# Attention chunks of 480, 480, 448 and 448 queries, a spread of the v and z preparation, and later read-back of the logits, in an attention and mixture-of-experts kernel

## The chip, the cores and the metric

One core of a Trainium2 chip runs the whole kernel. The metric is device time in microseconds (us). The engines are TensorE (PE, with its weight loads as PEld), VectorE (DVE), ScalarE (ACT), GpSimd (POOL) and SyncE (SP), which issues most of the DMAs.

## The reference

Eight batches of 1856 positions with 256 features: an attention without softmax, multiplied with `u`, and then a mixture of experts (MoE) with 4 groups of 4 experts over all 14848 rows.

```python
scores = z @ z.T / S                      # z: (8, 1856, 64)
attn = np.maximum(scores, 0.0) ** 2
x = (u * (attn @ v)).reshape(N, 256)      # N = 14848
g_idx = argmax(x @ w_group)               # g_w, e_w: softmax weights of the chosen
e_idx = argmax(x[g_idx == g] @ w_expert[g])
h = np.maximum(x @ w1[g, e], 0.0)         # 256 -> 1024
out = g_w * e_w * (h @ w2[g, e])          # 1024 -> 256
```

## The kernel before

**Precision.** Every product runs in split form: a value is cut into a high part, which ACT or DVE rounds to the matmul's type, and a low part, which DVE forms as the difference. So `v` becomes `vh` and `vl` (L246, L247), `z` becomes `z2h` and `z2l` (L215, L216), and the attention weights become `ah` and `al` (L275, L278).

**Attention** (about 10 to 892 us) runs over 8 batches, 4 query chunks and 15 key blocks of 128 keys (the last one holds 64 keys, high and low part packed together). The chunks are the list `QW`: 512, 512, 512 and 320 queries, from the offsets `QO`. One step `s` is one key block of one chunk. Keys are numbered through: step 60·b + 15·c + k is key k of chunk c in batch b, and names such as `al_293` carry that number. `scores(s)` makes two matmuls into a PSUM bank (L265, L266), with `zm`, the chunk's own queries, as the moving operand; ACT takes the relu (L268) and the square (L274), DVE casts `ah` and subtracts `al`. For the keys in `ACT_TWICE` ACT squares twice and DVE has no cast. `attn_v(s)` makes six matmuls (L295, L296, L298) into two accumulating banks, four for the last key. `scores` runs five steps (`LEAD`) ahead of `attn_v`.

**The end of a chunk** (`chunk_end`): DVE multiplies with `u` (`xT`), ACT and DVE cut the result (`xh`, `xl`), ACT copies it into 16-bit planes (`pl`, L336), SP transposes these with DMAs into `rows` (L342). Four matmuls make the routing logits (L350, L351), ACT copies them to `lgp` (L355), SP transposes them by DMA to `lgx` (L358), and DVE copies them back to `lgf` (L364, `logits_tr`, deferred by 5 steps). From there the generator `route` yields small DVE operations, three per step, makes three small matmuls and ends with POOL's scatters of rows into DRAM buckets (L480). A chunk whose width is no multiple of 128 has a partial tile: POOL then clears the rest of `pl` and `lgp` (L328, L329), and planes and `lgp` are copied in two pieces.

**Preparation of the next batch.** `prep_z` loads a block of 512 (the last: 320 and the tail) columns of z (L208, L210) and later cuts it; `prep_v` loads 512 rows of v (L234, L240) and later cuts them; `prep_zm` copies the queries of the next chunk from `z2h` and `z2l` to `zm` (L225, L226). Rings of buffers bound how early that can be: two for raw v, two for raw z, which `lgp` shares, sixteen for cut v (two batches).

**Batch 0** has 16 prefills besides (L661, one for each expert's bucket, 1280 rows of 264 words, 1.35 MB each), which SP issues.

**What sets the order.** A scheduler with a cost model orders each engine's instructions within the dependencies and the rings, so the place in the program is a wish: loads and cuts of v and z go where their buffers come free.

**The MoE** (from about 892 us) runs expert by expert in blocks of up to 512 rows: `phase1` (L616 to L618) with the block's width as columns, `phase2` (L639, L640). The change doesn't touch it.

Of the kernel before, what the change touches and what calls it, by code (L numbers as in the profile page):

```python
# [19 lines left out]
P = 128  # L20
# [4 lines left out]
def f32(ap):  # L25
    return ap.bitcast(F32)
# [3 lines left out]
def tile_glu_attn_moe(  # L30
# [19 lines left out]
    TAIL = S - NKF * P  # L50
    NK = NKF + 1
    assert TAIL == 64 and DQ == 64 and ND == 2 and NE == 16
    NQ = 4
    QW = [512, 512, 512, S - 1536]
    QO = [0, 512, 1024, 1536]
    assert all(cv % 16 == 0 and cv >= 2 * P for cv in caps)
    assert 256 <= QW[3] and QW[3] + TAIL <= 512
    RW = D + 8
    RU = 2 * RW
    CAPB = (N + 511) // 512 * 512 + 512  # L60
# [40 lines left out]
    def bank(pl, tag, name):  # L101
        return pl.tile([P, 512], F32, tag=tag, name=name)

    bucket = tc.dram_tile([NROW + OVT, RW], I32, name="bucket")
    views = dram_disjoint_views(bucket, B * NK)

    padrow = cst("padrow", [P, RW], I32)
    nc.gpsimd.memset(padrow, 0)
# [6 lines left out]
        out=tri, in_=tri, compare_op=ALU.is_gt, fill=0.0, base=0,  # L115
# [73 lines left out]
    def defer(step, fn):  # L189
        deferred.append((step, fn))  # L190
# [8 lines left out]
    bz = {}  # L199
# [1 line left out]
    zms = {}  # L201

    def prep_z(b, c):
        q0, w = QO[c], QW[c]
        wx = w + (TAIL if c == NQ - 1 else 0)
        zr = sb("zr", [P, 512], F32, 2, f"zr_{b}_{c}")
        for h in range(2):
            nc.sync.dma_start(zr[h * DQ:(h + 1) * DQ, 0:w], zT[b, :, q0:q0 + w])  # L208
            if wx > w:
                nc.sync.dma_start(zr[h * DQ:(h + 1) * DQ, w:wx], zT[b, :, S - TAIL:S])  # L210

        def split():
            z2h = new_z(f"z2h_{b}_{c}")
            z2l = new_z(f"z2l_{b}_{c}")
            nc.scalar.copy(out=z2h[:, 0:wx], in_=zr[:, 0:wx])  # L215
            nc.vector.tensor_sub(out=z2l[:, 0:wx], in0=zr[:, 0:wx], in1=f32(z2h[:, 0:wx]))  # L216
            bz[(b, c)] = (z2h, z2l)

        return split

    def prep_zm(b, c):
        w = QW[c]
        z2h, z2l = bz[(b, c)]
        zm = sb("zm", [P, 512], F32R, 2, f"zm_{b}_{c}")
        nc.vector.tensor_copy(out=zm[0:DQ, 0:w], in_=f32(z2h[0:DQ, 0:w]))  # L225
        nc.vector.tensor_copy(out=zm[DQ:P, 0:w], in_=f32(z2l[DQ:P, 0:w]))  # L226
        zms[(b, c)] = zm

    def prep_v(b, c):
        n = min(4, NK - 4 * c)  # L230
        nfull = min(n, NKF - 4 * c)
        raw = new_stg(f"vr_{b}_{c}")
        rv = raw.rearrange("p (k d) -> p k d", d=D)
        nc.sync.dma_start(  # L234
            rv[:, 0:nfull, :],
            v[b, 4 * c * P:(4 * c + nfull) * P, :].rearrange("(k p) d -> p k d", p=P),
        )
# [12 lines left out]
        return split  # L250
# [140 lines left out]
    def route(b, c, rows, lg, nt, part):  # L391
        NG = nt * 5

        def t(tag, shape, dt=F32):
# [29 lines left out]
            out=oh16.rearrange("p i (g e) -> p i g e", e=4),  # L424
# [13 lines left out]
        for _ in range(4):  # L438
# [10 lines left out]
            out=rk, in0=pk[:, 0:W].rearrange("p (i e) -> p i e", e=NE),  # L449
# [128 lines left out]
    wts = {}  # L578
# [90 lines left out]
    pz = prep_z(0, 0)  # L669
    pv = prep_v(0, 0)  # L670
# [20 lines left out]
    for s in range(NS):  # L691
        b, c, k = steps[s]
        if s == 1:
            pv1()
        if s in (0, 4):
            n0 = s // 4 + 2
            pz1 = prep_z(0, n0)
            pv2.append(prep_v(0, n0))
        if s in (2, 6):
            pz1()  # L700
        if s in (5, 9):
            pv2.pop(0)()
        if b == 0 and s >= 10 and s % 2 == 0 and s < 10 + 2 * NE:
            prefill((s - 10) // 2)
        nxt = s // NK + 1
        if k == 0:
            if nxt < B * NQ:
                load_ut(nxt // NQ, nxt % NQ)
            if b + 1 < B:
                if c < NQ - 1:  # L710
                    pv = [prep_v(b + 1, c)]
            else:
                if c == 0:
                    wts[0] = new_w("e0")
                pv = []
                if c:
                    pv = [load_w(regs(0)[0], wts[0], c - 1, "e0")]
                if c == NQ - 1:
                    pv.append(load_w(regs(0)[0], wts[0], c, "e0"))
        for zc, zb, lc, lk, sk in ((0, b + 1, 2, 0, 4), (1, b + 1, 3, 0, 4), (2, b + 1, 3, 6, 10), (3, b, 0, 0, 4)):  # L720
            if c == lc and 0 < zb < B:
                if k == lk:
                    pz = prep_z(zb, zc)
                if k == sk:
                    pz()
        if k == 12 and b + 1 < B and c == NQ - 2:
            pv.append(prep_v(b + 1, NQ - 1))
        if k in (11, 13) and pv:
            pv.pop(0)()
        if k == 8 and nxt < B * NQ and (nxt // NQ, nxt % NQ) in bz:  # L730
# [12 lines left out]
        run_gens(s, 3)
# [52 lines left out]
    def ot(shape, name, dt=F32):  # L796
# [24 lines left out]
        out=big, in0=exc.unsqueeze(2).to_broadcast([P, NE, TOV]),  # L821
# [115 lines left out]
```

## Time and profile before

| what | value |
|---|---|
| median of three runs | 1595.3 us (1595.13 to 1595.54) |
| the profiled execution, its own time | 1597.17 us |
| its span in the profile | 1595.3 us |
| attention, from the trace | about 10 to 892 us |
| MoE | about 892 us to the end |
| mean granted clock of PE | 0.993 |

A window of the trace gives, for a stretch, each engine's busy time and number of instructions. Since matmuls are pipelined, a full PE shows as busy throughout; where an engine is below the length of its stretch, it waited. The timeline gives each instruction with the idle time ahead of it and what released it, in square brackets.

### The profile page before, as it was taken

To read this page: it belongs to the slowest core of one execution; us is meant where nothing else is said; L and a number is where in the kernel's file an instruction comes from. 1 tells how busy PE (TensorE), PEld (TensorE's weight loads), DVE (VectorE), ACT (ScalarE), POOL (GpSimd) and SP (SyncE) were. 2 spreads that over 40 slices of the span, in tenths; PEclk is the share of its full clock that TensorE was granted. 3 is DMA by queue.
4 is the path that set the end of the run, shared out by engine and by line. 5 is a ranking of instruction groups with operands and counts; after the bars stand their busy time and mean duration, and the time that the engine had idled before them with its cause. 6 is when DMAs were issued, how large, how long until landed. Compare 5 with 4: busy or idle time off the path is not lost.

```text
span 1595.3 us, 23282 instructions
## 1 busy us (share of the span) xinstructions
PE 1549.9 (97%) x7808; PEld 1311.1 (82%) x7808; DVE 1081.1 (68%) x2539; ACT 1000.0 (63%) x1886; POOL 273.0 (17%) x323
## 2 busy tenths in 40 slices
PE   8998989999999999999999999999999999999998
PEld 5777877878878878878888798988888888888887
DVE  6868777787787786878787846555555555555572
ACT  6877778887787878787888535344444444444432
POOL 0003211111121211121202321112112222111211
PEclk9999999999999999999999999999999999999999
DMA  8794233233151333231332454233333433333200
GB/s 262 245 297 138 73 89 82 78 104 82 45 142 45 88 102 77 81 85 48 93 91 68 122 109 126 81 100 106 100 96 92 103 102 89 83 91 112 78 23 20
DMA packets 245115, 161.55 MB, mean 101 GB/s; under 512 B 168939, under 2 KB 224243, under 8 KB 244992
## 3 DMA queue, kind: packets, MB, share of 16 engines
q1 hardware_dynamic: 233296, 129.14, 31.8%
q0 software_dynamic: 11696, 30.90, 5.7%
q8 instruction: 62, 1.02, 0.3%
q14 instruction: 61, 0.50, 0.1%
HBM read 72.50 MB, written 53.59 MB: 79 GB/s over the span
## 4 chain that ended last, share of the span: by engine, by line
PE 77%; issue 6%; DVE 5%; ACT 5%; DMA 4%; SPq 2%; POOL 1%; POOLq 0%; ACTq 0%; DVEq 0%
PE py L639 13%; PE o L295 9%; PE o L296 9%; PE o L298 9%; PE py L640 7%; PE ph L617 6%; PE ph L616 6%; PE ph L618 6%; PE sc L265 5%; PE sc L266 5%; DMA lgx<-lgp 1%; SPq L661 1%; ACT r L268 1%; DVE al L278 1%; ACT r L274 1%
## 5 line engine op out<-in xcount | busy, mean ns | idle before, releaser
L295 PE MATMUL o<-ah,vl 128*128 128x512 f32 (+1 forms) x960 | 358.8, 375 | 12.1 <-DVE ah L275 12.1
L296 PE MATMUL o<-ah,vh 128*128 128x512 f32 (+1 forms) x960 | 356.8, 373 | 0.0
L639 PE MATMUL py<-w_e,hh 128*128 128x512 f32 (+3 forms) x1024 | 348.3, 394 | 0.0
L268 ACT ACTIVATE r<-sc 128x512 f32<-128x512 f32 (+1 forms) x480 | 255.7, 554 | 123.8 <-PE sc L266 86.6
L278 DVE TENSOR_TENSOR al<-r,ah 128x512 fp32r<-128x512 f32 (+1 forms) x448 | 285.2, 638 | 39.0 <-ACT r L272 31.8
L298 PE MATMUL o<-al,vh 128*128 128x512 f32 (+1 forms) x896 | 279.8, 378 | 17.8 <-DVE al L278 17.5
L640 PE MATMUL py<-w_e,hl 128*128 128x256 f32 (+4 forms) x1024 | 264.7, 280 | 0.1
L622 DVE SCALAR_TENSOR_TENSOR hl<-ph,hh 128x512 fp32r<-128x512 f32 (+10 forms) x288 | 175.0, 615 | 119.8 <-ACT hh L621 119.3
L621 ACT ACTIVATE hh<-ph 128x512 fp32r<-128x512 f32 (+10 forms) x288 | 153.5, 538 | 151.7 <-PE ph L618 150.0
L480 POOL DMA_INDIRECT bucket<-rows,di x120 | 127.6, 1063 | 564.0 <-issue 245.7
L647 POOL DMA_INDIRECT out_dram<-y,meta x128 | 129.4, 1011 | 552.3 <-DVE y L645 526.7
L295 PEld LDWEIGHTS o<-ah,vl 128*128 128x128 f32 x960 | 182.5, 190 | 48.7 <-DVE ah L275 19.3
L274 ACT ACTIVATE r<-r 128x512 f32<-128x512 f32 (+1 forms) x384 | 219.5, 591 | 3.1
L639 PEld LDWEIGHTS py<-w_e,hh 128*128 128x128 f32 (+3 forms) x1024 | 181.4, 185 | 36.7
L617 PE MATMUL ph<-xh_m,w1h_e 128*128 128x512 f32 (+10 forms) x576 | 207.7, 361 | 0.0
L616 PE MATMUL ph<-xh_m,w1l_e 128*128 128x512 f32 (+10 forms) x576 | 207.4, 360 | 0.0
L298 PEld LDWEIGHTS o<-al,vh 128*128 128x128 f32 x896 | 164.5, 191 | 52.2 <-DVE al L278 26.3
L618 PE MATMUL ph<-xl_m,w1h_e 128*128 128x512 f32 (+10 forms) x576 | 206.3, 361 | 0.0
L296 PEld LDWEIGHTS o<-ah,vh 128*128 128x128 f32 x960 | 182.5, 190 | 28.3
L640 PEld LDWEIGHTS py<-w_e,hl 128*128 128x128 f32 (+4 forms) x1024 | 187.6, 185 | 11.3 <-DVE hl L622 0.5
L275 DVE CAST ah<-r 128x512 fp32r<-128x512 f32 (+1 forms) x384 | 152.1, 399 | 55.8 <-ACT r L274 55.5
L265 PE MATMUL sc<-zm,z2h 128*128 128x512 f32 (+1 forms) x480 | 180.7, 384 | 6.6 <-ACT r L268 4.8
(140 smaller groups left out, 1862.2 us busy)
## 6 DMA issues: line engine op xcount, KB each, us to landing
raw_e<-in_w_dram SPq DMA_DIRECT2D x64, 512.0 KB, 3.9
bucket<-padrow SPq DMA_DIRECT2D x16, 1320.0 KB, 14.0
vr<-in_v_dram SPq DMA_DIRECT2D x24, 512.0 KB, 4.7
ut<-in_uT_dram SPq DMA_DIRECT2D x24, 512.0 KB, 4.0
zr<-in_zT_dram SPq DMA_DIRECT2D x48, 128.0 KB, 2.7
ut<-in_uT_dram SPq DMA_DIRECT2D x8, 320.0 KB, 3.2
vr<-in_v_dram SPq DMA_DIRECT2D x8, 256.0 KB, 3.4
out_dram<-y,meta POOLq DMA_INDIRECT x128, 2.4
```

What stands on the lines that cost most here:

```text
L265: nc.tensor.matmul(ps[:, 0:w], z2h[:, ks], zm, start=True, stop=False)
L268: nc.scalar.activation(out=a, in_=ps[:, 0:w], func=AF.Relu, scale=1.0 / S)
L274: nc.scalar.activation(out=a, in_=a, func=AF.Square)
L278: nc.vector.tensor_sub(out=al, in0=a, in1=f32(ah))
L295: nc.tensor.matmul(o, vl[:, dsl], ah, start=(k == 0), stop=False)
L296: nc.tensor.matmul(o, vh[:, dsl], ah, start=False, stop=(k == NK - 1))
L298: nc.tensor.matmul(o, vh[:, dsl], al, start=False, stop=False)
L616: nc.tensor.matmul(o, wt["l"][d][:, fs], xh[:, d, 0:W], start=(d == 0), stop=False)
L617: nc.tensor.matmul(o, wt["h"][d][:, fs], xh[:, d, 0:W], start=False, stop=False)
L618: nc.tensor.matmul(o, wt["h"][d][:, fs], xl[:, d, 0:W], start=False, stop=(d == ND - 1))
L639: nc.tensor.matmul(py[0:m], hh[:, ts], w2t, start=(f == 0), stop=False)
L640: nc.tensor.matmul(py[0:m, 0:D], hl_[:, ts], w2t[:, 0:D], start=False, stop=(f == NF - 1))
```

## The change

The four chunks become 480, 480, 448 and 448 wide, from 0, 480, 960 and 1408. The z blocks keep their 512 columns (`ZW`), so that `prep_zm` copies a chunk's queries out of one or two z blocks in two to four pieces. Every chunk now has a partial tile, of 96 or 64 rows, and four row tiles. `ACT_TWICE` goes from three keys to two. The loads and cuts of the next batch's v and z follow the table `PREP`, whose entries are a kind, a block, and two places (chunk, key) for load and cut. The logits' copy `lgf` is deferred by 8 steps in place of 5, except for the very last chunk. In the views for the scatters each chunk has `NT` = 4 of its own.

```diff
-    QW = [512, 512, 512, S - 1536]
-    QO = [0, 512, 1024, 1536]
+    QW = [480, 480, 448, 448]
+    QO = [0, 480, 960, 1408]
+    ZW = [512, 512, 512, S - 1536]
...
-    ACT_TWICE = (3, 7, 11)
+    ACT_TWICE = (4, 10)
+    NT = 4
...
 def prep_z(b, c):
-        q0, w = QO[c], QW[c]
+        q0, w = 512 * c, ZW[c]
...
 def prep_zm(b, c):
+        q = QO[c]
+        while q < QO[c] + QW[c]:
+            n = min(512 * (q // 512 + 1), QO[c] + QW[c]) - q
+            z2h, z2l = bz[(b, q // 512)]
+            src, dst = slice(q % 512, q % 512 + n), slice(q - QO[c], q - QO[c] + n)
+            nc.vector.tensor_copy(out=zm[0:DQ, dst], in_=f32(z2h[0:DQ, src]))
+            nc.vector.tensor_copy(out=zm[DQ:P, dst], in_=f32(z2l[DQ:P, src]))
+            q += n
...
-        defer(s + 5, logits_tr)
-        gens.append((max(s + 6, 42), g))
+        wait = 5 if last else 8
+        defer(s + wait, logits_tr)
+        gens.append((max(s + wait + 1, 42), g))
...
-                out=views[b * NK + 4 * c + i],
+                out=views[(b * NQ + c) * NT + i],
...
+    PREP = (
+        ("v", 0, (0, 1), (0, 7)), ("v", 1, (0, 9), (1, 3)), ("v", 2, (1, 5), (1, 10)), ("v", 3, (1, 12), (2, 4)),
+        ("z", 0, (1, 6), (1, 12)), ("z", 1, (2, 6), (2, 12)), ("z", 2, (3, 5), (3, 11)), ("z", 3, (3, 6), (3, 13)),
+    )
...
+        if b + 1 < B:
+            for what, n, load, cut in PREP:
+                if (c, k) == load:
+                    prep[(what, n)] = (prep_v if what == "v" else prep_z)(b + 1, n)
+                if (c, k) == cut:
+                    prep.pop((what, n))()
```

In the fourth chunk of batch 4 (keys 285 to 299), stands the copy of the logits of chunk 2. First DVE's order before:

```order
L364 COPY lgf_4_2_6667<-lgx_4_2_6561 128x4x2x40
L278 TENSOR_TENSOR al_293_6639<-r_293_6634,ah_293_6636 128x320
L367 TENSOR_TENSOR lg_4_2_6562<-lgf_4_2_6667 128x80
L247 TENSOR_TENSOR vl_6_1_7465<-vr_6_1_7237,vh_6_1_7464 128x1024
L403 TENSOR_REDUCE m_4_2_6686<-lg_4_2_6562 128x20
L216 TENSOR_TENSOR z2l_5_1_6648<-zr_5_1_6565,z2h_5_1_6647 128x512
L275 CAST ah_294_6656<-r_294_6654 128x320
L225 CAST zm_5_1_7079<-z2h_5_1_6647 64x512
L406 TENSOR_TENSOR d_4_2_6688<-lg_4_2_6562,m_4_2_6686 128x80
L226 CAST zm_5_1_7079<-z2l_5_1_6648 64x512
L278 TENSOR_TENSOR al_294_6659<-r_294_6654,ah_294_6656 128x320
```

And DVE's order at the same place now:

```order
L370 COPY lgf_4_2_6854<-lgx_4_2_6678 128x4x2x40
L373 TENSOR_TENSOR lg_4_2_6679<-lgf_4_2_6854 128x80
L410 TENSOR_REDUCE m_4_2_6876<-lg_4_2_6679 128x20
L284 TENSOR_TENSOR al_295_6809<-r_295_6804,ah_295_6806 128x448
L413 TENSOR_TENSOR d_4_2_6878<-lg_4_2_6679,m_4_2_6876 128x80
L418 TENSOR_SCALAR key_4_2_6882<-d_4_2_6878 128x80
L253 TENSOR_TENSOR vl_6_1_7445<-vr_6_1_7226,vh_6_1_7444 128x1024
L420 TENSOR_TENSOR key_4_2_6882<-key_4_2_6882,iota4_78 128x80
L281 CAST ah_296_6827<-r_296_6825 128x448
L471 TENSOR_REDUCE sm_4_2_7027<-ex_4_2_6880 128x20
L423 TENSOR_REDUCE km_4_2_6900<-key_4_2_6882 128x20
```

The copy moves two keys back (from key 293 to key 295), the z cut and the two zm copies are gone from behind it, and the value cut `vl_6_1` of batch 6 is still there.

On SP, in batch 0, stand the prefills (`bucket`), the loads and the first transposes; `lgx_0_0` is the transpose of the first chunk's logits. SP's order before (three prefills and one more stand ahead of these rows):

```order
L234 DMA vr_2_0_1504<-in_v_dram 128x4x256
L234 DMA vr_2_1_1872<-in_v_dram 128x4x256
L303 DMA ut_0_2_527<-in_uT_dram 128x2x512
L342 DMA_TRANSPOSE rows_0_0_521<-pl_0_0_523 128x4x128 x4
L358 DMA_TRANSPOSE lgx_0_0_525<-lgp_0_0_524 128x8x48
L661 DMA bucket_69<-padrow_70 1280x1x264 x7
```

And SP's order now, from the first prefill on:

```order
L668 DMA bucket_69<-padrow_70 1280x1x264 x3
L240 DMA vr_1_2_640<-in_v_dram 128x4x256
L240 DMA vr_1_3_771<-in_v_dram 128x2x256
L246 DMA vr_1_3_771<-in_v_dram 64x256 x2
L668 DMA bucket_69<-padrow_70 1280x1x264 x2
L210 DMA zr_1_0_658<-in_zT_dram 64x512 x2
L668 DMA bucket_69<-padrow_70 1280x1x264 x3
L240 DMA vr_2_0_1563<-in_v_dram 128x4x256
L240 DMA vr_2_1_1762<-in_v_dram 128x4x256
L309 DMA ut_0_2_533<-in_uT_dram 128x2x448
L668 DMA bucket_69<-padrow_70 1280x1x264
L348 DMA_TRANSPOSE rows_0_0_525<-pl_0_0_527 128x4x128 x4
```

Behind the last row comes `lgx_0_0`, so that nine prefills stand ahead of it in place of four, and two z loads of batch 1 as well.

On DVE the copy that waits for that transpose, `lgf_0_0`, stood here before:

```order
L278 TENSOR_TENSOR al_20_539<-r_20_534,ah_20_536 128x512
L275 CAST ah_21_556<-r_21_554 128x512
L278 TENSOR_TENSOR al_21_559<-r_21_554,ah_21_556 128x512
L364 COPY lgf_0_0_628<-lgx_0_0_525 128x4x2x40
L367 TENSOR_TENSOR lg_0_0_526<-lgf_0_0_628 128x80
```

And on DVE it stands here now:

```order
L284 TENSOR_TENSOR al_32_787<-r_32_782,ah_32_784 128x448
L281 CAST ah_33_801<-r_33_799 128x448
L370 COPY lgf_0_0_694<-lgx_0_0_529 128x4x2x40
L284 TENSOR_TENSOR al_33_804<-r_33_799,ah_33_801 128x448
L373 TENSOR_TENSOR lg_0_0_530<-lgf_0_0_694 128x80
```

It moved from behind key 21 into key 33, which is eleven to twelve keys later.

## Rows read from the trace of the kernel before

**Rows 1.** Page, part 1: busy time, share of the span, instructions.
```profile
PE 1549.9 (97%) x7808; PEld 1311.1 (82%) x7808; DVE 1081.1 (68%) x2539; ACT 1000.0 (63%) x1886; POOL 273.0 (17%) x323
```
**Rows 2.** Windows, batch 3's chunks: us, busy PE PEld DVE ACT POOL, clock, DMA, GB/s.
```profile
354.80:382.80 28.00, 27.70 (x125) 22.13 (x124) 24.32 (x69) 22.06 (x46) 6.45 (x8) 1.00 0.43 94
382.80:411.00 28.20, 28.20 (x127) 22.77 (x126) 20.44 (x57) 22.33 (x41) 1.94 (x3) 1.00 0.23 58
411.00:438.20 27.20, 27.20 (x127) 22.23 (x126) 20.34 (x58) 20.36 (x39) 3.77 (x5) 1.00 0.26 65
438.20:461.70 23.50, 21.02 (x127) 18.74 (x126) 18.52 (x54) 20.66 (x44) 5.06 (x7) 1.00 0.48 124
```
**Rows 3.** Windows: chunk 3 of batches 0, 1; chunk 0 of 2; chunk 3 of 2, 4, 6.
```profile
103.00:134.30 31.30, 23.88 (x133) 21.07 (x132) 22.59 (x73) 21.56 (x45) 7.61 (x10) 0.89 0.90 246
...
216.50:245.70 29.20, 24.69 (x131) 21.56 (x130) 20.24 (x59) 20.51 (x42) 5.58 (x6) 0.88 0.41 113
245.70:275.00 29.30, 28.18 (x128) 22.24 (x126) 23.71 (x69) 23.63 (x48) 4.32 (x6) 1.00 0.34 82
...
330.10:354.80 24.70, 22.25 (x127) 20.15 (x126) 18.75 (x54) 20.87 (x43) 4.20 (x6) 0.93 0.46 129
...
545.40:570.40 25.00, 22.51 (x127) 20.30 (x126) 19.15 (x55) 21.14 (x45) 5.20 (x7) 0.93 0.46 124
...
760.90:782.60 21.70, 20.72 (x128) 18.90 (x127) 15.98 (x51) 18.22 (x42) 4.72 (x7) 1.00 0.35 91
```
**Rows 4.** Timeline of DVE, chunk 3 of batch 3: start, us, instruction, idle before.
```profile
450.12 0.35 DVE L364 COPY lgf<-lgx 128x320 uint16<-128x320 uint16 x1 [0.90 <-DMA lgx<-lgp]
450.36 0.48 DVE L278 TENSOR_TENSOR al<-r,ah 128x320 fp32r<-128x320 f32 x1
...
450.92 1.22 DVE L247 TENSOR_TENSOR vl<-vr,vh 128x1024 fp32r<-128x1024 f32 x1
...
452.80 0.32 DVE L275 CAST ah<-r 128x320 fp32r<-128x320 f32 x1
```
**Rows 5.** Timeline of PE at the same place.
```profile
450.90 0.41 PE L298 MATMUL o<-al,vh 128*128 128x320 f32 x1 [0.68 <-DVE al L278]
```
**Rows 6.** Timeline of PE: ends of gapless stretches (512 and 320 attention; 320, 448, 480 MoE).
```profile
470.64 0.39 PE L295 MATMUL o<-ah,vl 128*128 128x512 f32 x1
...
481.52 0.39 PE L295 MATMUL o<-ah,vl 128*128 128x512 f32 x1
...
447.12 0.31 PE L295 MATMUL o<-ah,vl 128*128 128x320 f32 x1
...
449.47 0.31 PE L295 MATMUL o<-ah,vl 128*128 128x320 f32 x1
...
948.62 0.31 PE L616 MATMUL ph<-xh_m,w1l_e 128*128 128x320 f32 x1
...
955.66 0.39 PE L639 MATMUL py<-w_e,hh 128*128 128x512 f32 x1
...
1330.76 0.36 PE L616 MATMUL ph<-xh_m,w1l_e 128*128 128x448 f32 x1
...
1340.68 0.40 PE L639 MATMUL py<-w_e,hh 128*128 128x512 f32 x1
...
1243.82 0.38 PE L616 MATMUL ph<-xh_m,w1l_e 128*128 128x480 f32 x1
...
1254.22 0.40 PE L639 MATMUL py<-w_e,hh 128*128 128x512 f32 x1
```
**Rows 7.** Timeline of SP's queue in batch 0: start, us, transfers issued.
```profile
58.23 21.43 SPq L661 DMA_DIRECT2D bucket<-padrow  x7
```
**Rows 8.** Timelines of DVE and PE in batch 0: two read-backs, and PE behind one.
```profile
60.75 0.36 DVE L364 COPY lgf<-lgx 128x320 uint16<-128x320 uint16 x1 [3.17 <-DMA lgx<-lgp]
...
123.52 0.35 DVE L364 COPY lgf<-lgx 128x320 uint16<-128x320 uint16 x1 [3.26 <-DMA lgx<-lgp]
...
124.90 0.90 PE L298 MATMUL o<-al,vh 128*128 128x320 f32 x2 [4.10 <-DVE al L278]
```

More of the change, by code (lines that the diff above doesn't have):

```diff
@@ L53, in tile_glu_attn_moe @@
     NQ = 4
-    QW = [512, 512, 512, S - 1536]
-    QO = [0, 512, 1024, 1536]
+    QW = [480, 480, 448, 448]
+    QO = [0, 480, 960, 1408]
+    ZW = [512, 512, 512, S - 1536]
+    assert sum(QW) == S
     assert all(cv % 16 == 0 and cv >= 2 * P for cv in caps)
-    assert 256 <= QW[3] and QW[3] + TAIL <= 512
     RW = D + 8
@@ L104, in tile_glu_attn_moe @@
     bucket = tc.dram_tile([NROW + OVT, RW], I32, name="bucket")
-    views = dram_disjoint_views(bucket, B * NK)
+    views = dram_disjoint_views(bucket, B * NQ * NT)
     padrow = cst("padrow", [P, RW], I32)
@@ L221, in prep_zm @@
     def prep_zm(b, c):
-        w = QW[c]
-        z2h, z2l = bz[(b, c)]
         zm = sb("zm", [P, 512], F32R, 2, f"zm_{b}_{c}")
-        nc.vector.tensor_copy(out=zm[0:DQ, 0:w], in_=f32(z2h[0:DQ, 0:w]))
-        nc.vector.tensor_copy(out=zm[DQ:P, 0:w], in_=f32(z2l[DQ:P, 0:w]))
+        q = QO[c]
[6 more added lines that the diff above has]
+            q += n
         zms[(b, c)] = zm
@@ L685, in tile_glu_attn_moe @@
     pv2 = []
+    prep = {}
+    PREP = (
+        ("v", 0, (0, 1), (0, 7)), ("v", 1, (0, 9), (1, 3)), ("v", 2, (1, 5), (1, 10)), ("v", 3, (1, 12), (2, 4)),
+        ("z", 0, (1, 6), (1, 12)), ("z", 1, (2, 6), (2, 12)), ("z", 2, (3, 5), (3, 11)), ("z", 3, (3, 6), (3, 13)),
+    )
     xs = []
@@ L708, in tile_glu_attn_moe @@
                 load_ut(nxt // NQ, nxt % NQ)
[L709 to L712, printed above, removed]
+            if b + 1 == B:
                 if c == 0:
                     wts[0] = new_w("e0")
-                pv = []
+                pw = []
                 if c:
-                    pv = [load_w(regs(0)[0], wts[0], c - 1, "e0")]
+                    pw = [load_w(regs(0)[0], wts[0], c - 1, "e0")]
                 if c == NQ - 1:
[L719 to L730, printed above, removed]
+                    pw.append(load_w(regs(0)[0], wts[0], c, "e0"))
+        if b + 1 == B and k in (11, 13) and pw:
+            pw.pop(0)()
+        if b + 1 < B:
[4 more added lines that the diff above has]
+                    prep.pop((what, n))()
+        if k == 8 and nxt < B * NQ:
             prep_zm(nxt // NQ, nxt % NQ)
```

## The prediction

> **What bounds the kernel now.** I read the page's busy shares first: TensorE (PE) is busy 97% of the span [rows 1], so a change can gain only where PE waits or steps slower than it could, and it can lose by making PE's own work longer. Then I read the attention part chunk by chunk in a table of busy time by stretch [rows 2, 3]. The reader is to see two kinds of chunk. The wide ones are full: in batch 3, chunks 1 and 2 (512 queries) take 28.20 and 27.20 us and PE is busy in all of it, while DVE has 20.4 us of work there and ACT 20 to 22. The narrow fourth chunk (320 queries) is not: 23.50 us, with PE idle for 2.5 of it and stretched by waits that the busy column does not show.
>
> How long should it be? I take the price of a matmul as the distance between starts in stretches without a gap [rows 6]: 48 matmuls at 512 columns lie in 481.52 − 470.64 = 10.88 us, 0.2267 us each, and 16 at 320 columns in 2.35 us, 0.1469 each (in the MoE 7.04 us for 48, 0.1467). A chunk has 15 keys: 14 with 2 scores and 6 value matmuls, one with 2 and 4, so 118, and 4 for the logits. In the time of a fourth chunk 108 of these run at 320 columns and 14 at 512 (ten scores of the next chunk, which run five keys ahead, and the four logits of the chunk before): 108 × 0.1467 + 14 × 0.2267 = 19.0 us, and about 0.3 for the three small matmuls of the routing: **19.3 us**. The windows of batches 1, 2, 3, 4 and 6 are 29.2, 24.7, 23.5, 25.0 and 21.7 us [rows 2, 3], so they lose 9.9, 5.4, 4.2, 5.7 and 2.4; batch 5 has a window like batch 3's, 4.2. Sum 31.8 us over six batches. Part of it is clock: the granted clock falls to 0.88 and 0.93 of full in the chunks with the long waits, that is, PE runs on the lower of its two levels (1.2 against 2.4 GHz) for a while after a pause; (1 − 0.88) × 29.2 = 3.5 us in batch 1.
>
> Why there? The timeline of DVE shows it [rows 4]: DVE stands 0.90 us before the copy of the logits that come back from their transpose (lgf, a wait for a DMA), and right behind it comes a value cut of 1.22 us (vl); by the order below a z cut and two zm copies follow within eight rows more. PE then waits 0.68 us for `al` [rows 5]. At 320 columns PE uses up a key in 8 × 0.147 = 1.17 us, so a key's cut delayed by 2 us is more than the ring of keys carries; at 512 it has 1.81 us a key, and the same instructions in chunk 1 cost nothing [rows 2].
>
> **The change part by part.** I count against the span, 1595.3 us; the profiled execution's own time is 1597.17, 0.12% above the median of the runs, which is 1595.3 too. So the sum is made on 1595.3.
>
> *Chunks of 480, 480, 448, 448: the stalls.* The key of the fourth chunk becomes 8 × 0.2067 = 1.65 us (448 columns, [rows 6], below), close to the 1.81 of a wide chunk; its work on DVE grows too: cast and subtraction take 0.32 + 0.48 = 0.80 us a key at 320 columns [rows 4], at most 448/320 of it at 448, so DVE's work in the chunk goes from 18.5 [rows 2] to at most 18.5 + 15 × 0.32 = 23.3 us in some 25.6: 91%. The nearest row for such a load is chunk 0 of batch 3, where DVE has 24.32 of 28.00 us (87%) and PE idles 0.3 [rows 2]; the dearest is the 2.4 that batch 6 loses [rows 3]. Residual per batch between 0.1 (chunk 2 of batch 3) and 2.4; I take 1.0, nearer the loaded wide chunk. Gain 31.8 − 6 × 1.0 = **25.8 us** (bounds 17.4 and 31.2). In chunk 0 of batch 2, 29.30 us against some 27.7 without waits [rows 3], I count **1.5** more, since the same cuts reach into it.
>
> *The cuts of v and z.* The table spreads loads and cuts; the order shows that it moves z cuts and zm away from the logits copy (none stands within ten rows behind it now; before, z2l and both zm did), but a value cut still stands six rows behind it, since these go where a buffer comes free. What is left is one 1.2 us item behind one wait, in keys of 1.65 us. I count nothing beyond the stalls above; both ends are in their bounds. SP's moved loads (2 DMAs per z block, 4 for the last; 1 per v block, 3 for the last) pass a queue whose DMA engines are busy 23 to 48% [rows 2], so nothing.
>
> *The width price.* The same 1856 columns per batch are cut otherwise. If a matmul cost a fixed time per column, nothing would change, since the number of matmuls is the same. The rows say otherwise [rows 6]: at 448 columns 48 matmuls take 9.92 us, 0.2067 each, and at 480 columns 10.40 us, 0.2167; a straight line through 320 and 512 would give 0.2000 and 0.2133. Per batch: before 3 × 122 × 0.2267 + 122 × 0.1467 = 100.9 us; after 2 × 122 × (0.2167 + 0.2067) = 103.3. **+2.4 us a batch, +19.3** in eight. These prices come from the MoE; that the two 320 rows agree (0.1469 and 0.1467) is why I carry them over. Lower bound 0, upper 19.3.
> The Trainium skill ("TensorE: Matmul & The Clock Gate", section "Back-to-back issue gap") gives the isolated gap as N/2.4 + 2.5 ns, which is linear in N. By that the price would be nil and the sum 19.3 us lower. This trace disagrees with it: 10.9 ns above the formula at 512, 17.5 at 448, 14.2 at 480.
>
> *Longer read-back, 8 keys instead of 5.* In batch 0 DVE waits 3.26 us for the third chunk's logits, and PE 4.10 right behind [rows 8]. Three keys more are 3 × 1.65 = 5 us, more than the wait: **−4.1 us** (upper bound 0, if the landing moves too: these transfers share DMA engines that are 90% busy there [rows 3]). In later batches the waits are part of the stalls above. The last chunk keeps its 5.
>
> *Batch 0's first read-back.* Here the order moves something that the diff doesn't show: on SP nine prefills instead of four stand ahead of the first logits transpose. The seven prefills that SP issued behind it took 21.43 us, 3.06 each [rows 7]; five more make 15.3 us. DVE took the logits at 60.75 after a wait of 3.17 [rows 8], so it was there at 57.6 and the data at about 60.7. Afterwards the data is there at about 76.0. DVE comes to the copy 11 or 12 keys later, by the order behind the cast of key 33 instead of the subtraction of key 21: 11.5 keys of 1.65 to 1.73 us, less 22 keys that are each 0.08 us shorter, about 18 us, so at 75.6. A wait of half a microsecond against 3.17 before: **0** (bounds −1.5 and the third rival).
>
> *Small edits, counted at nothing:* one cast more on DVE per chunk (two keys instead of three square twice on ACT; 0.32 us at 320 columns), plane and logit copies in two pieces in every chunk, zm in up to four pieces, one scatter and one transpose more per batch, memsets on POOL (273 us busy of 1595 [rows 1]). They lie beside PE's work: DVE's 20.4 and ACT's 20.4 to 22.3 us in 27 to 28 of a wide chunk [rows 2]. If DVE were the bound, the cast alone would be 32 × 0.4 = 13 us.
>
> Sum: 1595.3 − 25.8 − 1.5 + 19.3 − 4.1 = **1583.2 us**.
>
> **The rivals.**
> *R1, width is free*: in attention the price follows the columns. For it: PE's weight loads differ between the two phases. Against: the two 320 rows agree. 1583.2 − 19.3 = 1563.9 us.
>
> *R2, the stalls stay (slower)*: the cuts of a later batch's v go where buffers come free, and that is still the end of a batch; DVE's work there rises by up to 4.8 us, and the wait for the read-back stays ahead of a value cut. Place: DVE in chunk 3 and the next chunk 0. Then only batch 0's gain and the width price are left: 1595.3 + 19.3 − 4.1 = 1610.5 us. It decides from where fewer than 19.3 − 4.1 = 15.2 of the 27.3 us go, that is, where a fourth chunk keeps over 3 us of waits. For it: the order; batch 6's chunk loses 2.4 even without a clock drop [rows 3]. Against: chunk 0 of batch 3 with the same load [rows 2].
>
> *R3, the prefills hold the first read-back*: if the five added prefills go at the rate at which the engines move data in batch 0's full stretch, 246 GB/s [rows 3], 5 × 1.35 MB take 27.5 us, and the logits land at 88.2 where DVE is at 75.6. 12.6 us of wait, and a clock drop like that of batch 1 (3.5): 1583.2 + 16.1 = 1599.3 us. Against: the 3.06 us each that SP took [rows 7].
>
> **How the numbers follow.** This kernel's runs can tell 0.2% (3.2 us) from no change: faster is below 1592.1, slower above 1598.5. Forecast 0.57 (1578 to 1592: the stalls' bounds, 31.2 and 17.4), R1 0.15, R2 0.15, R3 0.13 of which half is above 1598.5. Faster 0.57 + 0.15 = 0.72; slower 0.15 + 0.06, less 0.04 for the cases in which only half of R2's waits stay, 0.17; the same is the rest, 0.11. The range reaches from just under R1 up to 1598, and leaves out R2 and most of R3, 2 in 10.
>
> **What would show it.** In the profile after: fourth chunks of some 26 us with PE busy in all of it and the clock at 1.00; matmuls of attention at 0.207 and 0.217 us from start to start (R1: 0.200 and 0.213 or below); no wait over 1 us before the logits copy, in batch 0 either (R3: 10 us or more near 76 to 88 us); DVE's waits before `al` and `ah` under 1 us per chunk (R2: 3 us and more, now also in chunk 0). If attention ends at about 880 us instead of 892 with the MoE unchanged, the sum is right; wrong would be a gain that comes from the MoE, or a wide chunk that has begun to wait.

## The result and the profile after

The changed kernel takes 1572.4 us (median of 4 runs, 1571.2 to 1572.6) against 1595.2 for the kernel before (1594.6 to 1595.5). The ratio is 0.9852, with a 95% interval of 0.9838 to 0.9866: 1.5% faster. The forecast was 1583.2, with a range from just under 1563.9 to 1598; the gain is 23 us where 12 were forecast. The profiled execution of the kernel before took 1597.2 us, 1.9 more than its median, so that the two traces lie 24.4 us apart and the medians 22.8.

The page after, part 1, answers to [rows 1]:

```profile
PE 1548.6 (99%) x7808; PEld 1345.2 (86%) x7808; DVE 1103.8 (70%) x2651; ACT 997.2 (63%) x1926; POOL 295.0 (19%) x379
```

PE has as many instructions and nearly as much busy time as before, in a span of 1570.9 us in place of 1595.3: what went from the profile is idle time. The windows by chunk show where. First the fourth chunk of batch 1, then the four chunks of batch 3, then the fourth of batch 4 (columns as in [rows 2]):

```profile
209.10:234.90 25.80, 25.17 (x122) 22.23 (x122) 19.79 (x54) 21.60 (x43) 5.21 (x6) 1.00 0.44 116
...
340.60:367.70 27.10, 27.10 (x129) 22.55 (x129) 24.03 (x73) 22.44 (x45) 5.64 (x8) 1.00 0.38 97
367.70:394.40 26.70, 26.70 (x128) 22.80 (x127) 21.43 (x63) 20.42 (x42) 4.85 (x7) 1.00 0.27 64
394.40:419.10 24.70, 24.70 (x125) 22.47 (x124) 19.57 (x63) 19.86 (x43) 4.89 (x7) 1.00 0.27 71
419.10:444.80 25.70, 25.70 (x126) 23.11 (x125) 21.03 (x58) 22.26 (x46) 4.86 (x6) 1.00 0.46 118
...
523.80:548.80 25.00, 25.00 (x124) 22.81 (x123) 20.48 (x56) 22.68 (x46) 4.34 (x6) 1.00 0.43 114
```

The fourth chunks are full now: in batch 3 PE is busy in all of the 25.70 us, where it idled 2.5 of 23.50 [rows 2], and the granted clock no longer falls (1.00 in batch 1, where it was 0.88 [rows 3]). The other chunks have fewer columns and became shorter.

It helps to cut the kernel into three stretches: batch 0 (to the first value matmul of batch 1), batches 1 to 6, and the rest. For batches 1 to 6, first before and then after:

```profile
134.30:782.60 648.30, 629.95 (x3002) 520.40 (x3002) 501.52 (x1418) 516.85 (x1000) 107.00 (x128) 0.99 0.32 83
```

```profile
129.40:758.50 629.10, 627.36 (x3003) 544.88 (x3003) 521.34 (x1510) 516.68 (x1029) 126.53 (x174) 1.00 0.34 87
```

Batches 1 to 6 became 19.2 us shorter, and PE's idle time in them went from 18.4 to 1.7 us. Batch 0 ends at 129.4 in place of 134.3, 4.9 earlier. The rest, from the end of batch 6 to the start of PE's last matmul (1587.6 and 1563.1), takes 805.0 and 804.6 us. 19.2 + 4.9 + 0.4 is the whole 24.5 us by which that matmul comes sooner. In this rest, attention ends at 866.1 instead of 892.1, so batch 7 is 1.9 us shorter, and from there to the last matmul the kernel takes 1.5 us longer: the gain does not come from the MoE.

The idle column tells less than the whole, since the end of a matmul is modelled and short waits hide in the busy time. The distances between starts show them. In batches 1 to 6 the median distance is 0.147 us at 320 columns and 0.227 at 512 before, and 0.204 at 448 and 0.217 at 480 after. With every matmul at the median of its width PE would need 608.5 us before and 618.7 after. That leaves 39.8 us of waits and of lower clock before, and 10.3 after, and makes the width price 10 us in six batches (8 by the mean of the distances close to the median).

Three views after answer to steps of the forecast. **PE's price by width**, from gapless stretches: 80 matmuls of 448 columns, 92 of 448 in another chunk, 80 of 480:

```profile
505.96 0.36 PE L301 MATMUL o<-ah,vl 128*128 128x448 f32 x1
...
522.17 0.20 PE L451 MATMUL pk<-oh,tri 128*128 128x64 bf16 x1
...
81.32 0.37 PE L304 MATMUL o<-al,vh 128*128 128x448 f32 x1
...
100.33 0.37 PE L302 MATMUL o<-ah,vh 128*128 128x448 f32 x1
...
766.23 0.37 PE L301 MATMUL o<-ah,vl 128*128 128x480 f32 x1
...
783.58 0.20 PE L451 MATMUL pk<-oh,tri 128*128 128x64 bf16 x1
```

16.21 us by 80 is 0.2026, 19.01 by 92 is 0.2066, and 17.35 by 80 is 0.2169 us a matmul. So 448 columns cost 0.2067 as forecast in one place and 0.203 in another.

**DVE behind the logits copy** in chunk 3 of batch 3, the place of [rows 4]:

```profile
433.04 0.37 DVE L370 COPY lgf<-lgx 128x320 uint16<-128x320 uint16 x1 [1.49 <-DMA lgx<-lgp]
...
434.52 1.22 DVE L253 TENSOR_TENSOR vl<-vr,vh 128x1024 fp32r<-128x1024 f32 x1
...
435.76 0.17 DVE L230 CAST zm<-z2h 64x32 fp32r<-64x32 f32 x1
...
436.13 0.38 DVE L230 CAST zm<-z2h 64x448 fp32r<-64x448 f32 x1
```

The wait and the value cut behind it are still there, the wait even longer (1.49 us against 0.90), and the zm copies are there too; only the z cut is gone from behind the copy. PE waits for none of it here.

**Batch 0**: SP's prefills and the first logits transpose, then DVE's copies of the first and third chunk's logits, then PE behind the third (these answer to [rows 7] and [rows 8]):

```profile
44.12 7.62 SPq L668 DMA_DIRECT2D bucket<-padrow  x3
...
69.60 1.21 SPq L364 DMA_TRANSPOSE lgx<-lgp  x1
```

```profile
72.26 0.36 DVE L370 COPY lgf<-lgx 128x320 uint16<-128x320 uint16 x1 [0.77 <-DMA lgx<-lgp]
...
116.48 0.49 DVE L370 COPY lgf<-lgx 128x320 uint16<-128x320 uint16 x1 [3.39 <-DMA lgx<-lgp]
```

```profile
121.09 0.98 PE L304 MATMUL o<-al,vh 128*128 128x448 f32 x2 [1.68 <-DVE al L284]
```

The transpose behind nine prefills was issued at 69.60 and cost DVE 0.77 us. The wait for the third chunk's logits did not go: 3.39 us against 3.26.

### The profile page after: what moved, and what is told of

Read it like the earlier page. It is cut to its first block, busy times and chain, and to the rows that moved or that the text cites. A ratio compares the mean times of both kernels' runs of the same rounds, so it can differ in the third digit from the quotient of the medians.

```text
span 1570.9 us, 23671 instructions
## 1 busy us (share of the span) xinstructions
PE 1548.6 (99%) x7808; PEld 1345.2 (86%) x7808; DVE 1103.8 (70%) x2651; ACT 997.2 (63%) x1926; POOL 295.0 (19%) x379
## 4 chain that ended last, share of the span: by engine, by line
PE 49%; issue 4%; DMA 1%; DVE 1%; POOL 1%; SPq 0%; ACT 0%; POOLq 0%; DVEq 0%; ACTq 0%
PE py L646 13%; PE py L647 7%; PE ph L623 6%; PE ph L624 6%; PE ph L625 6%; PE o L301 3%; PE o L302 3%; PE o L304 2%; PE sc L271 1%; PE sc L272 1%; POOL out_dram L654 1%; DMA raw_e<-in_w_dram 1%; SPq L592 0%; DVE w1l_e L166 0%; PE pl L357 0%
## 5 line engine op out<-in xcount | busy, mean ns | idle before, releaser
L301 PE MATMUL o<-ah,vl 128*128 128x448 f32 (+1 forms) x960 | 361.1, 376 | 3.3 <-DVE ah L281 2.6
L302 PE MATMUL o<-ah,vh 128*128 128x448 f32 (+1 forms) x960 | 359.7, 375 | 0.0
L274 ACT ACTIVATE r<-sc 128x480 f32<-128x480 f32 (+1 forms) x480 | 258.6, 553 | 107.7 <-PE sc L272 67.7
L284 DVE TENSOR_TENSOR al<-r,ah 128x480 fp32r<-128x480 f32 (+1 forms) x448 | 285.5, 637 | 42.6 <-ACT r L278 27.2
L304 PE MATMUL o<-al,vh 128*128 128x480 f32 (+1 forms) x896 | 291.7, 377 | 4.8 <-DVE al L284 4.8
L280 ACT ACTIVATE r<-r 128x480 f32<-128x480 f32 (+1 forms) x416 | 239.5, 591 | 5.0
L487 POOL DMA_INDIRECT bucket<-rows,di x128 | 137.2, 1072 | 400.0 <-DVE di L466 336.8
L281 DVE CAST ah<-r 128x480 fp32r<-128x480 f32 (+1 forms) x416 | 166.7, 403 | 34.4 <-ACT r L280 30.1
L271 PE MATMUL sc<-zm,z2h 128*128 128x480 f32 (+1 forms) x480 | 182.0, 381 | 4.0 <-ACT r L274 2.3
```

Of the source, the lines that this page charges most:

```text
L271: nc.tensor.matmul(ps[:, 0:w], z2h[:, ks], zm, start=True, stop=False)
L274: nc.scalar.activation(out=a, in_=ps[:, 0:w], func=AF.Relu, scale=1.0 / S)
L280: nc.scalar.activation(out=a, in_=a, func=AF.Square)
L284: nc.vector.tensor_sub(out=al, in0=a, in1=f32(ah))
L301: nc.tensor.matmul(o, vl[:, dsl], ah, start=(k == 0), stop=False)
L302: nc.tensor.matmul(o, vh[:, dsl], ah, start=False, stop=(k == NK - 1))
```

## The experiments

The table gives the twelve experiments below the two kernels. The ratio (with its 95% interval) is against the kernel before on the same chip (1595.2 us beside the changed kernel, 1595.7 to 1596.2 beside the others). The other columns are from the profiled execution of each: the end of batch 0, the length of batches 1 to 6, and PE's idle time in those. They are single executions: that of the kernel before was 1.9 us above its median and that with the read-back after 8 keys alone 2.8 us below, so that differences of 2 or 3 us in these columns settle nothing.

| kernel | median us | ratio | batch 0 ends | batches 1 to 6 | PE idle there |
|---|---|---|---|---|---|
| before | 1595.2 | 1 | 134.3 | 648.3 | 18.4 |
| changed | 1572.4 | 0.9852 (0.9838 to 0.9866) | 129.4 | 629.1 | 1.7 |
| widths alone | 1587.4 | 0.9940 (0.9924 to 0.9957) | 136.6 | 636.3 | 8.2 |
| all but the widths | 1573.3 | 0.9855 (0.9838 to 0.9872) | 133.9 | 627.7 | 7.7 |
| changed, read-back after 5 | 1572.7 | 0.9846 (0.9829 to 0.9862) | 129.4 | 631.0 | 1.7 |
| read-back after 8 alone | 1594.1 | 0.9991 (0.9981 to 1.0000) | 133.7 | 644.7 | 17.9 |
| v and z places alone | 1588.5 | 0.9949 (0.9930 to 0.9968) | 134.2 | 640.4 | 12.6 |
| keys 4, 10 squared twice, alone | 1578.9 | 0.9892 (0.9875 to 0.9910) | 130.5 | 636.6 | 11.7 |
| v places alone | 1590.7 | 0.9968 (0.9956 to 0.9980) | 131.5 | 645.4 | 15.7 |
| z places alone | 1584.2 | 0.9930 (0.9909 to 0.9951) | 131.9 | 639.0 | 12.2 |
| before, keys 4, 7, 10 | 1600.8 | 1.0026 (1.0015 to 1.0038) | 133.6 | 653.1 | 19.4 |
| before, keys 3, 11 | 1586.7 | 0.9940 (0.9923 to 0.9957) | 131.5 | 644.1 | 14.2 |
| changed, keys 3, 7, 11 | 1577.6 | 0.9884 (0.9868 to 0.9901) | 128.5 | 634.4 | 5.8 |
| changed, 512, 512, 448, 384 | 1571.0 | 0.9845 (0.9829 to 0.9862) | 133.0 | 624.3 | 2.4 |

**The widths alone.**

```diff
-    QW = [512, 512, 512, S - 1536]
+    QW = [480, 480, 448, 448]     # with ZW, the copies of zm in pieces, and the views
```

> Only the chunk widths of the change (480, 480, 448, 448, with the z blocks left at 512 and the queries copied in pieces); places of the v and z preparation, the read-back after 5 keys and the three keys squared twice are as before. Theory W (the widths alone take the waits out of the narrow fourth chunk): batches 1 to 6 gain 19 us, batch 7 nothing, batch 0 loses about 1: 1577 us. Rival P (the spread preparation and the later read-back take the waits out, and the widths only cost their price of 1.5 to 2.4 us a batch): 1607 to 1614 us.

It came out between the two, at 1587.4: batches 1 to 6 gain 12.0 us, batch 0 ends 2.3 later. The widths do take the waits out of the fourth chunk, as the forecast had it. In that of batch 3 DVE stands 2.36 us before the logits copy, with a value cut right behind, and PE is idle nowhere:

```profile
446.07 0.37 DVE L370 COPY lgf<-lgx 128x320 uint16<-128x320 uint16 x1 [2.36 <-DMA lgx<-lgp]
446.32 1.22 DVE L253 TENSOR_TENSOR vl<-vr,vh 128x1024 fp32r<-128x1024 f32 x1
```

```profile
431.00:456.60 25.60, 25.60 (x126) 23.19 (x126) 21.05 (x52) 22.51 (x45) 4.94 (x7) 1.00 0.44 114
```

But waits remain elsewhere: chunk 0 is 28.2 us in the mean of batches 1 to 6, no shorter than before in spite of its 32 columns less. By distances between starts 18.9 of the 39.8 us of waits are left, so the widths alone remove 21.

**All but the widths.**

```diff
-    QW = [480, 480, 448, 448]
+    QW = [512, 512, 512, 320]     # on the changed kernel
```

> All of the change but the widths, which are 512, 512, 512 and 320 again. Theory W: the fourth chunks keep most of their waits (31.8 us in batches 1 to 6), only batch 0's read-back gains 4 us: about 1591 us. Rival P: the waits go and no price of widths is paid: about 1560 us.

This run contradicts the forecast's main step in part: without the new widths the kernel is as fast as with them (the intervals of the ratios cover each other). At 1573.3 it lies between W's 1591 and P's 1560. The window of batches 1 to 6:

```profile
133.90:761.60 627.70, 620.02 (x3002) 516.36 (x3001) 510.75 (x1440) 512.56 (x978) 112.70 (x132) 1.00 0.33 86
```

PE is busy 620.0 us where the changed kernel has 627.4, and idle 7.7 where that has 1.7. By distances between starts, which count the short waits too, it is 608.5 us of matmuls and 19.1 of waits against 618.7 and 10.3. So on top of the rest the widths cost 8 to 10 us of longer matmuls for 7 to 9 us of waits. Their other effects are a batch 0 that ends 4.5 us sooner and a rest that is 1.9 longer. DVE and PE at the known place of batch 3, chunk 3:

```profile
440.41 0.36 DVE L370 COPY lgf<-lgx 128x320 uint16<-128x320 uint16 x1 [1.45 <-DMA lgx<-lgp]
440.66 1.21 DVE L253 TENSOR_TENSOR vl<-vr,vh 128x1024 fp32r<-128x1024 f32 x1
...
441.94 0.41 DVE L230 CAST zm<-z2h 64x512 fp32r<-64x512 f32 x1
```

```profile
443.51 0.56 PE L304 MATMUL o<-al,vh 128*128 128x320 f32 x2 [0.45 <-DVE al L284]
```

At 320 columns the copy waits 1.45 us, a value cut and both zm copies follow, and PE still waits only 0.45. The z cut is not behind the copy. (In batches 1 and 2 the same order costs PE 1.9 and 2.0 us; the table below comes back to that.)

**The read-back after 8 keys**, undone in the changed kernel, and alone on the kernel before.

```diff
-        wait = 5 if last else 8
+        wait = 5
```

> The changed kernel with the logits read back after 5 keys as before. Theory W: batch 0 gives back the 4 us that were put down to the later read-back, other batches under 1 us each: 1576 to 1580 us. Rival (the later read-back is what takes the waits out of the fourth chunks): near 1590 us.

```diff
-        defer(s + 5, logits_tr)
-        gens.append((max(s + 6, 42), g))
+        wait = 5 if last else 8
+        defer(s + wait, logits_tr)
+        gens.append((max(s + wait + 1, 42), g))
```

> The kernel before with the logits read back after 8 keys, nothing else. Theory W: batch 0 gains 4 us, the fourth chunks a little: 1587 to 1591 us. Rival (the later read-back is what takes the waits out): 1570 to 1578 us.

Neither W nor the rival foresaw these. Undone, it costs nothing that can be measured in all (1572.7), and batch 0 ends at the same 129.4. Alone it gains 0.1% at an interval that reaches to no change, and in batch 0 the third chunk's wait stays, DVE first and then PE:

```profile
122.86 0.35 DVE L364 COPY lgf<-lgx 128x320 uint16<-128x320 uint16 x1 [2.82 <-DMA lgx<-lgp]
```

```profile
124.25 0.90 PE L298 MATMUL o<-al,vh 128*128 128x320 f32 x2 [3.67 <-DVE al L278]
```

3.67 us against 4.10 [rows 8]. The three keys are a place in the program, and the place in DVE's order is the scheduler's: the copy starts at 122.86 against 123.52 before. What its cost model took for the landing no run shows.

**The other edits apart.** Since widths and read-back were not needed, the places of the v and z preparation, both and each, and the two keys were tried by themselves. (The loops and lines of the kernel before that the two lists replace are left out here.)

```diff
+        ("v", 0, (0, 1), (0, 7)), ("v", 1, (0, 9), (1, 3)), ("v", 2, (1, 5), (1, 10)), ("v", 3, (1, 12), (2, 4)),
+        ("z", 0, (1, 6), (1, 12)), ("z", 1, (2, 6), (2, 12)), ("z", 2, (3, 5), (3, 11)), ("z", 3, (3, 6), (3, 13)),
```

> The kernel before with the places of v and z loads and cuts as in the changed kernel, and nothing else: widths, keys squared twice and the 5 keys of the read-back as before. Theory Z (the run without the new widths gained all by moving the preparation): 1573 to 1578 us. Rival T (it takes the two keys squared twice in place of three as well, since ACT is what is full in the narrow chunk): 1583 us or more.

```diff
-    ACT_TWICE = (3, 7, 11)
+    ACT_TWICE = (4, 10)
```

> The kernel before with two keys squared twice (4 and 10) in place of three (3, 7, 11), nothing else. Theory Z: ACT loses a square and DVE gains a cast per chunk, neither decides: 1593 to 1597 us. Rival T: several us of the fourth chunk's waits go: 1580 to 1588 us.

The v entries alone (the z loop as before):

> The kernel before with only the v loads and cuts at their new places. Theory Z (v cuts go where their buffers come free, whatever the place; it is the z cuts that had to leave the fourth chunk): 1592 to 1597 us. Rival V (the v cuts are what is moved out of the way): 1573 to 1580 us.

The z entries alone (the v code as before):

> The kernel before with only the z loads and cuts at their new places. Theory Z: 1575 to 1580 us. Rival V: 1592 to 1597 us.

Places alone gain 7 us and z places alone 11.5; v places alone gain 5, of which batches 1 to 6 hold 2.9. Z lies nearer than V in both of those runs, yet outside its range each time, by 4 us for the z places and by 1 for the v places. That the preparation was all, as theory Z had it, missed by 10 us. Rival T held for the places, and the keys came out 1 us below its range. The edit that the forecast had counted at nothing, two keys squared twice in place of three, is the largest by itself: 16.7 us, 11.7 of it in batches 1 to 6. The traces say how. With two keys, DVE and PE in chunk 3 of batch 3:

```profile
438.76 0.69 DVE L216 TENSOR_TENSOR z2l<-zr,z2h 128x512 fp32r<-128x512 f32 x1 [1.03 <-ACT z2h L215]
...
440.71 0.36 DVE L364 COPY lgf<-lgx 128x320 uint16<-128x320 uint16 x1 [1.02 <-DMA lgx<-lgp]
...
441.36 0.41 DVE L225 CAST zm<-z2h 64x512 fp32r<-64x512 f32 x1
441.78 0.43 DVE L226 CAST zm<-z2l 64x512 fp32r<-64x512 f32 x1
442.24 1.23 DVE L247 TENSOR_TENSOR vl<-vr,vh 128x1024 fp32r<-128x1024 f32 x1
```

```profile
441.49 0.56 PE L298 MATMUL o<-al,vh 128*128 128x320 f32 x2 [0.22 <-DVE al L278]
...
444.07 0.56 PE L298 MATMUL o<-al,vh 128*128 128x320 f32 x2 [0.97 <-DVE al L278]
```

The scheduler has put the z cut (z2l) ahead of the logits copy, and PE's waits are 1.2 us. Before they are 2.2 us, the 0.68 of [rows 5] and these two:

```profile
453.17 0.41 PE L295 MATMUL o<-ah,vl 128*128 128x320 f32 x1 [0.95 <-DVE ah L275]
...
454.62 0.56 PE L298 MATMUL o<-al,vh 128*128 128x320 f32 x2 [0.61 <-DVE al L278]
```

The fourth chunk takes 22.1 us in the mean of batches 1 to 6, against 24.6.

**Number or place of the squared keys?**

```diff
-    ACT_TWICE = (3, 7, 11)
+    ACT_TWICE = (4, 7, 10)
```

> The kernel before with three keys squared twice, as many as before, but at 4, 7 and 10 in place of 3, 7 and 11. The run with two keys at 4 and 10 gave 1578.9 us against 1595.7. Theory N (the number decides: one square less on a full ACT and its latency gone): 1592 to 1597 us. Theory L (their places decide): 1577 to 1585 us.

```diff
-    ACT_TWICE = (3, 7, 11)
+    ACT_TWICE = (3, 11)
```

> The kernel before with two keys squared twice, as in the changed kernel, but at two of the old places, 3 and 11. Theory N (the number decides): 1577 to 1583 us. Theory L (their places decide): 1590 to 1597 us. Neither holds if both this run and the one with keys 4, 7, 10 land on the same side.

The totals settle neither theory. Three keys at the new places are slower than before (1600.8), above both ranges and on N's side; two at the old places are faster (1586.7), between the ranges. The fourth chunk tells more. In the mean of batches 1 to 6 it takes 24.7 us with keys 3 and 11, as before; that kernel gained elsewhere, in chunk 0 (27.5 against 28.2) and in batch 0. Its DVE order at the known place, and PE behind it:

```profile
444.43 0.36 DVE L364 COPY lgf<-lgx 128x320 uint16<-128x320 uint16 x1 [2.24 <-DMA lgx<-lgp]
444.68 1.22 DVE L247 TENSOR_TENSOR vl<-vr,vh 128x1024 fp32r<-128x1024 f32 x1
...
445.96 0.69 DVE L216 TENSOR_TENSOR z2l<-zr,z2h 128x512 fp32r<-128x512 f32 x1
...
446.80 0.50 DVE L225 CAST zm<-z2h 64x512 fp32r<-64x512 f32 x1
```

```profile
446.94 0.41 PE L295 MATMUL o<-ah,vl 128*128 128x320 f32 x1 [2.02 <-DVE ah L275]
...
448.48 0.56 PE L298 MATMUL o<-al,vh 128*128 128x320 f32 x2 [0.69 <-DVE al L278]
```

The z cut stands behind the copy again, and PE waits 2.7 us. The granted clock falls too. The windows of this chunk with keys 3 and 11 and with keys 4 and 10:

```profile
431.60:457.50 25.90, 22.92 (x128) 20.33 (x127) 19.07 (x53) 19.63 (x41) 3.97 (x7) 0.93 0.44 124
```

```profile
428.20:450.30 22.10, 20.91 (x127) 18.81 (x126) 17.63 (x44) 19.46 (x41) 5.16 (x7) 1.00 0.52 139
```

ACT has the same work in both (19.63 and 19.46 us, 20.66 before [rows 2]), so ACT's load does not make the difference between the two.

This sorts the kernels with a fourth chunk of 320 columns, by their timelines of this chunk. In before, with read-back 8, with the v places, and with keys 4, 7, 10 or 3, 11, value cut, z cut and both zm copies stand behind the waiting copy, the clock falls (to 0.87 to 0.94) in two to five of the fourth chunks of batches 1 to 6, and these take 24.0 to 25.0 us in the mean. With the z places, with both places, with keys 4, 10, and in the kernel without the new widths the z cut is not among them, the clock falls in one of the six at most, and they take 21.0 to 22.4. No kernel lies between.

Chunk by chunk the z cut is not what decides, though. In batch 2 with keys 3 and 11 it stands ahead of the copy as well, and PE waits 2.18 us all the same, with a clock of 0.93 and a chunk of 24.7 us; batch 5 is like it:

```profile
336.86 0.35 DVE L364 COPY lgf<-lgx 128x320 uint16<-128x320 uint16 x1 [0.73 <-DMA lgx<-lgp]
337.10 0.41 DVE L225 CAST zm<-z2h 64x512 fp32r<-64x512 f32 x1
337.54 0.42 DVE L226 CAST zm<-z2l 64x512 fp32r<-64x512 f32 x1
338.00 1.23 DVE L247 TENSOR_TENSOR vl<-vr,vh 128x1024 fp32r<-128x1024 f32 x1
339.14 0.48 DVE L278 TENSOR_TENSOR al<-r,ah 128x320 fp32r<-128x320 f32 x1
```

```profile
339.68 0.56 PE L298 MATMUL o<-al,vh 128*128 128x320 f32 x2 [2.18 <-DVE al L278]
```

With keys 4 and 10 a key's subtraction `al` (440.96 to 441.44) stands right behind the copy; here the first comes at 339.14. What sorts the chunks of batches 2 to 5 is how soon DVE gets back to the keys: the time from the start of the copy to the end of the second `al` behind it, against PE's idle time at this place (from DVE's wait to 6 us behind the start of the copy).

| kernel, batches 2 to 5 | second `al` done after, us | PE idles, us |
|---|---|---|
| before, read-back 8, v places, keys 4, 7, 10 | 4.3 to 4.5 | 2.1 to 2.7 |
| keys 3, 11 | 3.6 or 4.8 | 2.2 to 3.0 |
| keys 4, 10 | 3.3 | 1.2 to 1.3 |
| z places, both places | 2.7 | 0.6 to 0.8 |

In all of these PE has no subtracted key left when the copy starts (keys that DVE has subtracted, less those whose `al` PE has begun on). In the kernel without the new widths the time is 3.8 us, and PE idles 2.0 in batch 2, where none is left either, but only 0.5 in batches 3 to 5, where one is. So the loss comes from the work between the waiting copy and the next keys, less the keys that PE has in hand; the z cut is 0.69 us of that work. The z places are enough by themselves to shorten it, and the two keys do it through the scheduler's order. The z places also take the z cut and its cast on ACT out of the chunk; that share was not separated. Why the scheduler's order turns with keys 4 and 10 but not with 3 and 11 was not tried.

**The three keys in the changed kernel.**

```diff
-    ACT_TWICE = (4, 10)
+    ACT_TWICE = (3, 7, 11)        # on the changed kernel
```

> The changed kernel with three keys squared twice, 3, 7 and 11, as before. If the parts stand in for one another, so that the waits of the narrow chunk go by any two of them, it loses little: 1573 to 1578 us. If the number of squares is worth 16 us by itself whatever else is done: 1586 to 1590 us.

1577.6 us, inside the first range: 5 of the 17 us that this edit is worth alone. The parts stand in for one another. In batches 1 to 6 widths, places, keys and read-back alone gain 12.0, 7.9, 11.7 and 3.6 us, 35.2 in sum, and together 19.2: in large part they remove the same waits.

**Other widths, a candidate.**

```diff
-    QW = [480, 480, 448, 448]
+    QW = [512, 512, 448, 384]     # on the changed kernel
```

> The changed kernel with widths 512, 512, 448 and 384. In the trace of before, matmuls at 512 and 384 columns (0.2267 and 0.1735 us) lie on the same line as 320, and only 448 lies above it. By the prices read in attention (0.2279, 0.2042, 0.2171 us at 512, 448, 480) PE's work is 101.7 us a batch in place of 102.8: 9 us less in eight batches, less what a key of 1.39 us gives back in waits (0 to 5 us): 1564 to 1569 us. If the width price is none: 1572 us or more.

```profile
133.00:757.30 624.30, 621.92 (x3002) 536.57 (x3001) 509.95 (x1456) 514.76 (x978) 104.65 (x126) 1.00 0.33 85
```

Batches 1 to 6 are the shortest of all, 4.8 us less than in the changed kernel: PE's work fell by 5.4 us and its idle time rose by 0.6. But batch 0 ends 3.6 us later, and the total, 1571.0 us, can't be told from the changed kernel's 1572.4. It missed the 1564 to 1569 that were expected of it by 2 us, through batch 0.

## Why the prediction was right, and where it was not

*What bounds the kernel*: right. PE's waits at the border of fourth and first chunk were the gain, as [rows 3 to 5] show.

*The stalls*: the size was right, and the cause was only one of two. Against the 27.3 us forecast, some 27 to 29 came off (the 19.2 us of batches 1 to 6 and the 8 to 10 of width price that they paid). That the 448-column key takes the waits out of the fourth chunk is borne out by the widths alone, which remove 21 us of waits. But the forecast put all of it on this key, and the other edits without it remove 21 as well (39.8 less 19.1) and leave the kernel as fast. The step that failed is "I count nothing beyond the stalls above" for the cuts of v and z: moving the z preparation was a cause of its own, worth 9.3 us in batches 1 to 6 with the z places alone.

*Small edits, counted at nothing*: wrong for the two squared keys in place of three, 16.7 us alone, and 5 when they are taken out of the changed kernel. The forecast costed the cast that this adds on DVE (0.3 to 0.4 us) and did not ask what the scheduler does with it. The term was no cost but a different order.

*The width price*: the mechanism was right and the size off, 2.4 us a batch where 1.4 to 1.7 was paid. The prices came from one MoE block per width; in attention 448 columns take between 0.2026 and 0.2066 us, 0.204 in the median. R1, that width is free, fell: PE needs 8 to 10 us more for the new widths. The formula of the Trainium skill ("TensorE: Matmul & The Clock Gate", section "Back-to-back issue gap") for the isolated gap would give, as an estimate, 0.1892 and 0.2025 at 448 and 480 columns. The trace stands 13 to 17 and 14 ns above it, and 11 at 512, so that some 3 to 6 ns of it are not linear.

*Longer read-back in batch 0*: wrong. The third chunk's wait is still 3.39 us, and PE's 1.68 behind it is the same (1.69) when the 8 keys are undone. That batch 0 ended 4.9 us sooner has another cause. Its end lies between 128.5 and 136.6 in the fourteen kernels, with loads, prefills and transposes in another order on SP in the two that were compared; what sets it stays open.

*The nine prefills*: right in the result, and in part by luck. The copy waited 0.77 us, and the 12.6 us of R3 did not come. But the logits were there at 72.3 and DVE at 71.5, where the forecast had 76.0 and 75.6: two errors of about 4 us that cancel. SP took 0.8 to 2.5 us for each of the nine (7.62 for the three shown above), where 3.06 were counted. *R2* (the stalls stay) fell: the fourth chunks are full.

Of the signs, the fourth chunks, the clock and an earlier end of attention came as said. "No wait over 1 us before the logits copy" did not: it is 1.49 us in batch 3 and 3.39 in batch 0, though PE lost nothing by the first.

So the forecast's sign was right, but the read-back and the small edits were wrong and the width price too high. The time lies below the 1578 to 1592 that the bounds of its own mechanism gave, and in the range because that reached down to R1, which did not come: that it held is partly luck. The two traces hold 12.3 us more gain than the forecast: 6.3 in batches 1 to 6 (the width price 4 to 6 less than the 14.4 forecast, the stalls up to 2 more than forecast), 3.2 in batch 0 (4.9 for 1.7 with its price), and 2.8 in batch 7 and the MoE (0.4 gained where a price of 2.4 stood and the waits of batch 7 were left out).

## What to carry to other kernels

Where a scheduler with a cost model sets the order, cost an edit by the order it produces, not by the instructions it adds: here two double squares per chunk in place of three gained more alone than the new tile widths, and in the trace a cut had moved from behind a DMA wait to ahead of it. Look for the instruction that waits for a DMA in an engine's order, and count how long the work behind it keeps the engine from what the bounding engine needs next, against the steps that the bounding engine has in hand. And when several edits aim at the same waits, they don't add: take each away from the finished version before paying for it, since here the widths cost 8 to 10 us of matmul time for 7 to 9 us of waits that were left. Price matmuls by the distance between their starts: in batches 1 to 6 before, the busy column showed 18.4 us of idle time, and the distances 39.8 us of waits and lower clock.

## What the runs showed of the hardware

Matmuls of 448 columns follow each other at 0.2026 us in one gapless stretch and 0.2066 in another of the same kernel, and those of 480 at 0.2169, above the line through 320 and 512 (0.2000 and 0.2133); why two spacings occur was not tried.

PE's idle time in a chunk does not tell by itself whether its clock falls: with read-back 8 alone PE idled 3.06 us in the fourth chunk of batch 2 at a granted clock of 1.00, and in the kernel before 2.45 us there at 0.93 [rows 3].
